# Weight padding split into two ordered steps, a rounding op in four parts, and one more skip on VectorE, in a planned attention + state-space kernel

## The chip, the cores and the metric

The kernel runs on one core of a Trainium2 chip. The metric is device time in microseconds, the median over repeated runs. The engines are TensorE (PE in the profile, with its weight loads as PEld), VectorE (DVE), ScalarE (ACT), GpSimd (POOL) and SyncE (SP); SP issues most of the DMAs. PSUM is where matrix products land; an "evacuation" is the copy of a product from PSUM to SBUF by ACT or DVE.

## The reference, cut to what matters

Two independent layers over 2048 positions of width 448; their outputs stand side by side.

```python
def _A_ref(x, wqkv, wo):                 # attention: each position sees 8 earlier ones, 2 apart
    qkv = (x @ wqkv).reshape(B, S, 3, 16, 28)
    idx = pos[:, None] - (jnp.arange(8) * 2)[None, :]
    logits = einsum("bhsd,bhswd->bhsw", q, k[idx]) * 28 ** -0.5    # masked where idx < 0
    o = einsum("bhsw,bhswd->bhsd", softmax(logits), v[idx])
    return o.reshape(B, S, 448) @ wo

def _B_ref(x, Lambda_re, Lambda_im, B_re, B_im, C_re, C_im, log_dt, Dskip):
    Lam_bar = exp(exp(log_dt) * Lam)                                # complex, 448 states
    for t in range(2048):
        h = Lam_bar * h + Bu[t]                                     # Bu = x @ B_bar
    y = 2.0 * einsum("blp,dp->bld", hseq, Cmat).real + x * Dskip

out = concatenate([A_ref, B_ref], axis=-1)
```

## The kernel before, in words

**Positions go in pairs.** Inputs are viewed as 1024 rows of two positions each (even and odd), 896 numbers wide, and turned so that the width lies on partitions: 7 slabs of 128. With the attention's step of 2, even positions only see even ones and odd only odd. A weight of 448 rows does not divide into slabs of 128, and the two positions of a row start at different partitions, so weights are stored in 7 slabs too, with shifted copies of the same rows in the other 64 partitions (`Wv`, `Wpad`, `wo`); `pair` then runs two matmuls of 64 rows each at once, on upper and lower partitions (lines 546 and 547).

**Steps and their names.** Each step is a node with a name, a cost, its dependencies and a rank. The prediction uses these:

- `vw0..2` build the shifted half of `Wv`; `xt`, `xe` turn the first two blocks of x on PE and copy them out.
- `v0..v7` project V for eight blocks of 128 pairs (`v3_` is the first half of `v3`, four of its seven matmul pairs); `ev0..7` evacuate them.
- `wp{q}{z}` (function `n_wp`, lines 511 to 519) lays the weights of K (q=1) or Q (q=0), half z of the heads, out in 32 columns a head: five copies on one engine, from `Wraw` to `Wpad`. Lines 515 and 516 place the rows, 517 to 519 the copies shifted by 64 partitions.
- `q{q}{s}{c}` projects K or Q for four heads s and chunk c (0: pairs 0 to 255, 1: to 511, 2: to 1023); `eq...` evacuates it.
- `s{par}{b}` scores of block b for even (0) or odd (1) positions, two PSUM units; `x{par}{b}0/1` their exponentials on ACT (line 750); `a{b}` the product with V; `n{b}` the division on DVE.
- `t0`, `tk`, `ts`, `t2`, `t3`, `t4` make the table of sines and cosines: angles on ACT (`t0`), rounding on DVE (`tk`, `ts`), sine on ACT (`t2`), absolute value on DVE (`t3`, line 454), cosine on ACT (`t4`, line 457). The exponentials wait for `t4`.
- `l1`, `l2` scale the B matrices (`wtmp`, `natW`); their transposes by DMA are `WT`.
- `b{hf}{k}` products for one half of the sequence, `be` their evacuation, then on DVE `ma` (line 815), `ri`, `sc` (the scan, line 833), `mb`, `ro` (lines 840, 841): the states h.
- `cg`, `ch` scale C; `g0`, `g1` a Gram-like product `Gm`, evacuated by `ge0`, `ge1`.
- `w0..w7` the attention's output projection. `y{t}` (even) and `z{t}` (odd) the state-space output of block t, `ye` their evacuation, `yo` the store. For t = 4, 5, 6 the odd row's skip term is added on DVE (line 1036) from a product `xd{t}` made beforehand (line 955, from the load `xn` at lines 948 and 949); for the other t it is a matmul with a diagonal. The last odd row is done in two pieces, `z70` (320 columns) and `z71` (128), lines 1014 and 1017.
- `gu1..3` a guard that decides at the end whether a slow exact path runs.

**What sets the order.** `Plan.run` is a list scheduler at build time: it takes the nodes in order of rank, keeps a clock for each engine from the written costs, and gives a free engine the first node that is ready. The result is a fixed order of instructions on each engine, and each engine runs its list in order; real waits are semaphores. So a change of a rank, of a cost or of an earliest time (`at`) moves instructions. PSUM is four units (`mm`), given out in a ring in PE's order: a step needs the unit of the fourth one before it to have been evacuated. A half of `pair` work is followed by a small GpSimd write (`tick`, line 554) that the second half waits for.

Of the kernel before, what the change touches and what calls it, by code (L numbers as in the profile page):

```python
# [23 lines left out]
SCALE = float(DH) ** -0.5  # L24


RANK = {"vi": (-544.75, 131.055), "v": (-110.39, 34.569), "q0": (63.48, 25.419), "q1": (-1326.93, 228.142), "s": (-380.99, 73.488), "a": (-188.15, 159.093),
        "b0": (56.3, -31.172), "b1": (2986.12, -242.123), "d0": (94.79, 241.448), "d1": (1628.45, -108.947), "l": (2486.1, 164.979), "t": (251.37, -53.356),
        "tk": (731.53, 100.376), "xd": (2178.91, -29.053), "cg": (593.37, 8.672), "ch": (1143.63, -50.034), "g": (436.44, 143.698), "y": (468.94, 183.089),
        "w": (1186.02, 1.256), "gu": (1304.36, -293.628), "q2": (430.19, -21.545), "wp": (-27.3, 132.469)}  # L30


class Plan:


    WAKE, TURN = 0.13, 0.1

    def __init__(self, pools):
        self.nodes, self.pools = [], pools
# [177 lines left out]
def kernel(  # L217
# [24 lines left out]
    def t_(shape, dt, name, tag=None):  # L242
        return sb.tile(shape, dt, tag=tag or name, name=name)
# [33 lines left out]
    def xbar_x(dst, src, lo, hi):  # L277
        SP.dma_start_transpose(dst[:, :, lo:hi], src[lo:hi, :])
# [8 lines left out]
    xn_ = [Pb[i][:].rearrange("p a b c -> p (a b c)")[:, 0:2 * D] for i in range(2)]  # L287
    SP.dma_start(xn_[0], xA2[0:128, :])
    ACT.dma_start(Wv[:, 0:3, :], wmain(2))
    ACT.dma_start(Wv[0:64, 3, :], A_wqkv[384:448, 2 * D:3 * D])  # L290
    SP.dma_start(xn_[1], xA2[128:256, :])
    for i, vec in ((2, B_Lambda_im), (3, B_Dskip)):
        G.dma_start(rows[7 * i:7 * i + 7, :], vec.rearrange("(c p) -> c p", p=64))
# [14 lines left out]
    SP.dma_start(Pt[0:64, :], B_B_im[384:448, :])  # L308
    SP.dma_start(Pt[64:128, :], B_B_re[384:448, :])
    xbar_x(xB, xB2, 0, 256)  # L310
    xbar_x(xB, xB2, 256, 512)


    def sel(o, i, pat, op, fill, base, ch):
# [136 lines left out]
        ACT.activation(tab[:, 1], ang, ACTF.Sin, scale=-2 * PI * SHR)  # L451

    def n_t3(e):
        V.tensor_scalar(ang.bitcast(I32), ang.bitcast(I32), 0x7FFFFFFF, None, ALU.bitwise_and)

    def n_t4(e):
        ACT.activation(tab[:, 0], ang, ACTF.Sin, bias=hpi[:], scale=-2 * PI * SHR)
# [33 lines left out]
    def n_vw(e, i):  # L491
        if i == 0:
            V.tensor_copy(Wv[64:128, 4:6, :], Wv[0:64, 1:3, :])
            V.tensor_copy(Wv[64:128, 3, :], Wv[0:64, 0, :])
        elif i == 1:
            V.tensor_copy(Wv[64:128, 6, :], Wv[0:64, 3, :])
        else:
            V.tensor_copy(Wv[0:64, 4:7, :], Wv[64:128, 0:3, :])

    def n_xt(e, i, h):  # L500
        h["ps"] = unit()
        tp = h["tp"] = h["ps"][:].rearrange("p a b -> p (a b)").bitcast(BF16)
        for k in range(7):
            PE.transpose(tp[:, 1024 * (k // 4) + 128 * (k % 4):1024 * (k // 4) + 128 * (k % 4) + 128], xn_[i][:, 128 * k:128 * k + 128], eye[:])
# [6 lines left out]
    def n_wp(e, q, z):  # L511
        o = Wpad[:, :, q, 256 * z:256 * z + 256].rearrange("p k (h c) -> p k h c", c=32)[:, :, :, 0:DH]
        i = Wraw[:, :, D * q + 224 * z:D * q + 224 * z + 224].rearrange("p k (h c) -> p k h c", c=DH)
        f = V.tensor_copy if e == "V" else ACT.copy
        f(o[:, 0:3], i[:, 0:3])
        f(o[0:64, 3], i[0:64, 3])
        f(o[64:128, 3], i[0:64, 0])
        f(o[0:64, 4:7], i[64:128, 0:3])
        f(o[64:128, 4:7], i[0:64, 1:4])

    def evac(e, o, i):
        if e == "A":
            ACT.copy(o, i)  # L523
        else:
            V.tensor_copy(o, i)  # L525
# [58 lines left out]
    late = 18.0  # L584
    gm = []
    for i, f in enumerate(gms):
        gm.append(node(f"gm{i}", {"G": 0.45}, f, gm[-1:], 4))
    g_1 = [node(f"one{a}", {"G": 0.67}, lambda e, a=a: g_one(e, a), [], 10, at=late) for a in range(2)]
    g_z = [node(f"zer{i}", {"G": 0.33 if i < 3 else 0.5}, lambda e, i=i: g_zero(e, i), [], 11, at=late) for i in range(4)]
    g_r = node("rcs", {"G": 0.35}, g_rcs, [], 14, at=late)  # L590
# [21 lines left out]
        tk_ = node(f"tk{k}", {"V": 0.53}, lambda e, k=k: n_tk(e, k), [pB, g_i] + (tss[k - 2:k - 1] if k > 1 else []), ("tk", k))  # L612
        tss.append(node(f"ts{k}", {"V": 0.62}, lambda e, k=k: n_ts(e, k), [t0, tk_], ("t", 0)))
    t2 = node("t2", {"A": 1.9}, n_t2, tss + [e2], ("t", 0))
    t3 = node("t3", {"V": 1.2}, n_t3, [t2], ("t", 0))
    t4 = node("t4", {"A": 2.0}, n_t4, [t3], ("t", 0))
    dg = [node(f"dgO{k}", {"G": 0.5}, lambda e, k=k: g_dgO(e, k), [pD], 15, at=45.0) for k in range(4)]
    for k in range(4):
        dg.append(node(f"dgE{k}", {"G": 0.5}, lambda e, k=k: g_dgE(e, k), [pD] + gm + dg[4:], 15, at=45.0))
    vw = []  # L620
    for i in range(3):
        vw.append(node(f"vw{i}", {"V": (0.48, 0.18, 0.44)[i]}, lambda e, i=i: n_vw(e, i), vw[-1:], (-400, -399, -397)[i], at=(4.5, 5.3, 5.3)[i]))
    xr = []
    for i in range(2):
        h = {}
        x = node(f"xt{i}", {"P": 0.6}, lambda e, i=i, h=h: n_xt(e, i, h), [g_e], -500, alloc="mm", at=(4.3, 5.0)[i])
        xr.append([node(f"xe{i}{z}", {"A": (0.49, 0.37)[z], "V": (0.6, 0.47)[z]}, lambda e, i=i, z=z, h=h: n_xe(e, i, z, h), [x], -398,
                        frees=[(x, 0)]) for z in range(2)])
    wp = {(q, z): node(f"wp{q}{z}", {"V": 1.55, "A": 2.9}, lambda e, q=q, z=z: n_wp(e, q, z), [g_p], ("wp", 2 * z + 1 - q), at=9.7 if q else 11.8)
          for z in range(2) for q in (1, 0)}  # L630


    MS = (0, 4, 1, 5, 2, 6, 3)
# [305 lines left out]


    outv = out[0].rearrange("(t two) n -> t two n", two=2)
    YD = (4, 5, 6)
    sk = {}
    sdone = [n for n in plan.nodes if n["name"][0] == "s" and n["name"][1] in "01"]

    def n_xn(e):
        xo = sk["x"] = t_([128, 4, D], BF16, "xo", "Kt")
        SP.dma_start(xo[:, 0:3, :], B_x[0].rearrange("(b t two) d -> t b two d", two=2, t=128)[:, YD[0]:YD[2] + 1, 1, :])
        SP.dma_start(xo[:, 3, :], B_Dskip.partition_broadcast(128))
    xl = node("xn", {"S": 1.2}, n_xn, sdone, 25, lat=3.0)  # L950
# [34 lines left out]
    for t in range(8):  # L985
# [21 lines left out]
            for k in range(3):  # L1007
                PE.matmul(ps[:, 1, 64 + 128 * k:192 + 128 * k], xB[:, 4 + k, tk], dgO[:, 1 + k, :], start=False, stop=(k == 2), skip_group_check=True)

        def piece(e, lo, n, ds, tk=tk, h=h):  # L1010
            ps, hb = unit(), hbuf(1)
            h["z", lo] = ps
            for m in range(7):
                PE.matmul(ps[:, 1, 0:n], hb[:, m, 385:513], lazy["C1"][:, m, lo:lo + n], start=(m == 0), stop=False, skip_group_check=True)  # L1014
            for k in ds:
                a, b = (0, 64) if k == 0 else (128 * k - 64, 128 * k + 64)
                PE.matmul(ps[:, 1, a - lo:b - lo], xB[:, 3 + k, tk], dgO[:, k, 0:b - a], start=False, stop=(k == ds[-1]), skip_group_check=True)
# [13 lines left out]
        if t < YD[0]:  # L1031
            n2 = node(f"ye{t}", ab(2 * D), lambda e, ev=ev: ev(e, 0, 2), [n1] + qdone, r, frees=[(n0, 0)])
            node(f"yo{t}", {"S": 0.6}, lambda e, st=st: st(e, 0, 2), [n2], 60 + 3 * t, lat=2.2)
        elif t in YD:
            def add(e, t=t, h=h):
                V.tensor_tensor(h["o"][:, 1], h[1][:, 1, 0:D], sk["d"][:, t - YD[0], :], ALU.add)  # L1036
            n2 = node(f"ye{t}0", ab(D), lambda e, ev=ev: ev(e, 0, 1), [n0] + qdone, r, frees=[(n0, 0)])
            n3 = node(f"ye{t}1", {"V": 0.6}, add, [n1, n2, xd[t]], r, frees=[(n0, 0)])
            node(f"yo{t}", {"S": 0.6}, lambda e, st=st: st(e, 0, 2), [n3], 60 + 3 * t, lat=2.2)
        else:  # L1040
            n2 = node(f"ye{t}0", ab(D), lambda e, ev=ev: ev(e, 0, 1), [n0] + qdone, r, frees=[(n0, 0)])
            node(f"yo{t}0", {"S": 0.6}, lambda e, st=st: st(e, 0, 1), [n2], 60 + 3 * t, lat=2.2)
            for i, (lo, n, ds) in enumerate(((0, 320, (0, 1, 2)), (320, 128, (3,)))):
                n0 = n1 = node(f"z{t}{i}", {"P": (1.15, 0.52)[i]}, lambda e, lo=lo, n=n, ds=ds, piece=piece: piece(e, lo, n, ds),
                               [n0] + c1, (r[0], r[1], -0.1), alloc="mm")
                n3 = node(f"ye{t}{1 + i}", {"VA"[i]: (0.42, 0.2)[i]}, lambda e, lo=lo, n=n, h=h: evac(e, h["o"][:, 1, lo:lo + n], h["z", lo][:, 1, 0:n]),
                          [n1, n2], r, frees=[(n1, 0)])
                node(f"yo{t}{1 + i}", {"S": 0.5}, lambda e, lo=lo, n=n, tk=tk, h=h: SP.dma_start(outv[tk, 1, D + lo:D + lo + n], h["o"][:, 1, lo:lo + n]),
                     [n3], 61 + i + 3 * t, lat=2.2)
            g2["deps"].append(n1)  # L1050


    ps = unit()
    for i in range(7):
        PE.matmul(ps[:, 0, :], zz[:, 0:128], zz[:, 128:640], start=True, stop=True)
    plan.run({"P": 4.3, "A": 4.5, "V": 1.0, "S": 23.2, "G": 2.7})
    bad = nc.values_load(flag[0:1, 0:1])
    main.close()
    with tc.If(bad > 0, label="exact"):
# [31 lines left out]
```

## Time and profile before

| what | value |
|---|---|
| median of 13 runs | 134.47 us (134.07 to 136.32) |
| the profiled execution's own time | 134.16 us |
| its span | 132.4 us, so 1.76 us lie around it |
| PE busy | 126.1 us, 95% |
| DVE busy | 107.6 us, 81% |
| ACT busy | 90.2 us, 68% |
| POOL busy | 27.7 us, 21% |
| granted TensorE clock | 0.997 |

The profiled execution is 0.31 us below the median. A sum made from the profile is a difference against 134.16, and is carried over to the median unchanged. Busy shares are averages: what bounds a stage is read from the waits and the timeline of that stage. Matmuls are pipelined, so a stretch in which PE is shown busy can still hold small gaps between the starts of its rows.

### The profile page before, as it was taken

To read this page: it belongs to the slowest core of one execution; us is meant where nothing else is said; L and a number is where in the kernel's file an instruction comes from. 1 tells how busy PE (TensorE), PEld (TensorE's weight loads), DVE (VectorE), ACT (ScalarE), POOL (GpSimd) and SP (SyncE) were. 2 spreads that over 40 slices of the span, in tenths; PEclk is the share of its full clock that TensorE was granted. 3 is DMA by queue.
4 is the path that set the end of the run, shared out by engine and by line. 5 is a ranking of instruction groups with operands and counts; after the bars stand their busy time and mean duration, and the time that the engine had idled before them with its cause. 6 is when DMAs were issued, how large, how long until landed. Compare 5 with 4: busy or idle time off the path is not lost.

```text
span 132.4 us, 3803 instructions
## 1 busy us (share of the span) xinstructions
PE 126.1 (95%) x1533; PEld 70.9 (54%) x1533; DVE 107.6 (81%) x193; ACT 90.2 (68%) x121; POOL 27.7 (21%) x108
## 2 busy tenths in 40 slices
PE   5899999999999999999999999999999999999980
PEld 2455766786445454545454554655675655455550
DVE  0439999899879999999999999999999899921130
ACT  0539899989998956999999899834775266211120
POOL 6975146210899600000000000000000000000000
PEclk9999999999999999999999999999999999999998
DMA  4999989609848999442505123379346669442231
GB/s 78 310 261 224 214 185 231 121 7 114 168 81 150 186 182 127 100 115 42 130 5 111 21 63 75 107 225 119 107 99 175 146 66 296 139 139 74 69 104 45
DMA packets 42432, 17.26 MB, mean 130 GB/s; under 512 B 33452, under 2 KB 42412, under 8 KB 42412
## 3 DMA queue, kind: packets, MB, share of 16 engines
q1 hardware_dynamic: 41840, 16.58, 60.1%
q10 hardware_dynamic: 508, 0.40, 1.0%
q8 instruction: 13, 0.21, 0.6%
q14 instruction: 7, 0.06, 0.1%
q0 software_dynamic: 64, 0.00, 0.0%
HBM read 4.08 MB, written 3.67 MB: 58 GB/s over the span
## 4 chain that ended last, share of the span: by engine, by line
PE 86%; DMA 3%; ACT 3%; DVE 2%; issue 1%; POOL 0%; SPq 0%; POOLq 0%; ACTq 0%
PE mm L546 28%; PE mm L804 17%; PE mm L996 8%; PE mm L1003 7%; PE mm L763 5%; PE mm L998 5%; PE mm L895 4%; PE mm L740 4%; PE mm L547 3%; DMA P<-in_A_x_dram 3%; PE mm L744 3%; PE mm L1014 1%; ACT wtmp L529 1%; DVE Va L525 1%; ACT P L750 1%
## 5 line engine op out<-in xcount | busy, mean ns | idle before, releaser
L750 ACT ACTIVATE P<-mm 128x896 bf16<-128x896 f32 (+1 forms) x36 | 31.5, 929 | 2.1 <-PE mm L744 1.9
L546 PE MATMUL mm<-xA,Wpad 64*128 64x256 bf16 (+1 forms) x168 | 27.2, 305 | 0.4 <-POOL tick L554 0.4
L547 PE MATMUL mm<-xA,Wpad 64*128 64x256 bf16 (+1 forms) x168 | 27.2, 306 | 0.1
L523 ACT CAST ys<-mm 128x896 bf16<-128x896 f32 (+2 forms) x15 | 11.3, 765 | 23.1 <-PE mm L1003 8.9
L804 PE MATMUL mm<-xB,WT 128*128 128x512 bf16 x98 | 22.5, 379 | 0.2 <-PE mm L744 0.2
L554 POOL MEMSET tick<- 1x1 f32 x40 | 4.8, 120 | 83.6 <-PE mm L547 83.4
L546 PEld LDWEIGHTS <-Wpad 64*128 64x128 bf16 x168 | 14.9, 94 | 8.9 <-POOL tick L554 1.4
L547 PEld LDWEIGHTS <-Wpad 64*128 64x128 bf16 x168 | 14.7, 94 | 1.2 <-issue 0.5
L804 PEld LDWEIGHTS <-WT 128*128 128x128 bf16 x98 | 9.1, 97 | 10.8 <-issue 0.7
L546 PE MATMUL mm<-Wv,xA 64*128 64x448 bf16 x56 | 12.5, 350 | 0.0
L547 PE MATMUL mm<-Wv,xA 64*128 64x448 bf16 x56 | 12.4, 350 | 0.0
L996 PE MATMUL mm<-C,h 128*128 128x448 bf16 x56 | 11.9, 353 | 0.0
L546 PE MATMUL mm<-wo,OT 64*128 64x448 bf16 x56 | 10.8, 349 | 0.0
L547 PE MATMUL mm<-wo,OT 64*128 64x448 bf16 x56 | 10.8, 349 | 0.0
L1003 PE MATMUL mm<-C,h 128*128 128x448 bf16 x49 | 10.4, 353 | 0.0
L770 DVE TENSOR_TENSOR O<-mm,rcs 112x896 bf16<-112x896 f32 (+1 forms) x9 | 9.8, 1091 | 0.3
L523 ACT CAST u<-mm 128x1024 bf16<-128x1024 f32 (+1 forms) x8 | 7.2, 903 | 3.2 <-PE mm L804 3.2
L833 DVE TENSOR_TENSOR_SCAN rs<-p_r,ini,rv 128x512 bf16<-128x512 f32 x7 | 8.7, 1270 | 0.0
L833 DVE TENSOR_TENSOR_SCAN rs<-p_r,rv 128x512 bf16<-128x512 f32 x7 | 8.5, 1230 | 0.0
L763 PEld LDWEIGHTS <-P 128*128 128x128 bf16 x288 | 7.9, 96 | 1.0 <-issue 0.4
L1036 DVE TENSOR_TENSOR ys<-mm,xd 128x448 bf16<-128x448 f32 x3 | 1.9, 625 | 8.1 <-ACT ys L523 8.1
L815 DVE TENSOR_TENSOR ra<-u,tab 128x2048 bf16<-128x2048 bf16 x6 | 7.3, 1221 | 0.7 <-DVE h L841 0.5
(178 smaller groups left out, 242.5 us busy)
## 6 DMA issues: line engine op xcount, KB each, us to landing
out_dram<-ys SPq DMA_DIRECT2D x15, 224.0 KB, 2.4
Wraw<-in_A_wqkv_dram SPq DMA_DIRECT2D x2, 336.0 KB, 4.0
wo<-in_A_wo_dram SPq DMA_DIRECT2D x2, 336.0 KB, 3.1
P<-in_A_x_dram SPq DMA_DIRECT2D x2, 224.0 KB, 3.7
vw<-Va SPq DMA_DIRECT2D x2, 203.0 KB, 3.7
vw<-Va SPq DMA_DIRECT2D x2, 174.0 KB, 3.2
Wv<-in_A_wqkv_dram ACTq DMA_DIRECT2D x1, 336.0 KB, 4.0
natW<-in_B_B_re_dram SPq DMA_DIRECT2D x1, 336.0 KB, 4.8
```

Source lines behind the costliest of these rows:

```text
L523: ACT.copy(o, i)
L546: x = PE.matmul(ps[:, a, 0:n], lhs(0, lo[i]), rhs(0, lo[i]), start=(i == 0), stop=(i == 6), skip_group_check=True)
L547: y = PE.matmul(ps[:, b, 0:n], lhs(64, hi[i]), rhs(64, hi[i]), start=(i == 0), stop=(i == 6), skip_group_check=True)
L750: ACT.activation(P[:].rearrange("p s g q -> p g s q")[:, 2 * z:2 * z + 2, :, 0:n], h["s"][z][:, :, 0:4 * n].rearrange("p g (s q) -> p g s ...
L763: PE.matmul(av[:, par, 29 * hd:29 * hd + 29], hb_[par]["P"][:, hd // 4, hd % 4, :], v[:, par, hd, :], start=True, stop=True)
L770: V.tensor_tensor(O[0:n, :].rearrange("p (a h d) -> p a h d", a=2, h=H), avv[0:n, :, :, 0:DH], rc.unsqueeze(3).to_broadcast((n, 2, H, DH)) ...
L804: PE.matmul(ps[:, i, :], WT[:, j, 128 * m:128 * m + 128], xB[:, j, HALF * hf:HALF * hf + HALF], start=(j == 0), stop=(j == 6))
L815: V.tensor_tensor(a[:], x[:].unsqueeze(1).to_broadcast((128, 2, 2, HALF)), tab[:, :, k, :].unsqueeze(2).to_broadcast((128, 2, 2, HALF)), A ...
L833: V.tensor_tensor_scan(h["s"][:, i], p["r2"][:, k:k + 1].to_broadcast((128, HALF)), h["v"][:, i], 0.0 if hf == 0 else ini[:, m:m + 1], ALU ...
L996: PE.matmul(ps[:, 0, 0:D], hb[:, m, lo:lo + 128], lazy["C2"][:, m, :], start=(m == 0), stop=False, skip_group_check=True)
L998: PE.matmul(ps[:, 0, 0:D], xB[:, k, tk], Gm[:, k, :], start=False, stop=(k == 3), skip_group_check=True)
L1003: PE.matmul(ps[:, 1, 0:D], hb[:, m, lo + 1:lo + 129], lazy["C1"][:, m, :], start=(m == 0), stop=(t in YD and m == 6), skip_group_check=True)
```

## The change

1. `n_wp` keeps the two copies that place the rows; a new function `n_ws` makes the three shifted copies from `Wpad` itself, in runs of 256 columns, padding included, as a node of its own that follows its padding and may run on the other engine.
2. `n_t3` becomes four instructions, one for each 512 columns.
3. The odd skip of block 7 goes to DVE: a fourth row in the load `xn`, a product `xd7`, two additions with `xd7` in place of two copies, and no diagonal matmuls in `piece`. The last store is issued by ACT, not by SP.
4. The last 64 rows of `Wv` are loaded through POOL's queue, ahead of its other loads, not through ACT's; one transposing load of 256 rows becomes two of 128.
5. All ranks, some costs and earliest times and the planner's wake-up cost differ, and a table `FINE` adds an offset to the rank of about 240 single nodes. Through these the order of nearly every engine's list moves.

```diff
-RANK = {"vi": (-544.75, 131.055), "v": (-110.39, 34.569), ...
+RANK = {"vi": (-6211.57, 311.074), "v": (-394.68, 85.971), ...
+FINE = {"t0": -138.5, "tk0": -130.6, "ts0": 246.9, ...
-    WAKE, TURN = 0.13, 0.1
+    WAKE, TURN = 0.18, 0.1
...
-    ACT.dma_start(Wv[0:64, 3, :], A_wqkv[384:448, 2 * D:3 * D])
+    G.dma_start(Wv[0:64, 3, :], A_wqkv[384:448, 2 * D:3 * D])
...
-    xbar_x(xB, xB2, 256, 512)
+    xbar_x(xB, xB2, 256, 384)
+    xbar_x(xB, xB2, 384, 512)
...
     def n_t3(e):
-        V.tensor_scalar(ang.bitcast(I32), ang.bitcast(I32), 0x7FFFFFFF, None, ALU.bitwise_and)
+        for k in range(4):
+            V.tensor_scalar(ang[:, k].bitcast(I32), ang[:, k].bitcast(I32), 0x7FFFFFFF, None, ALU.bitwise_and)
...
         f(o[:, 0:3], i[:, 0:3])
         f(o[0:64, 3], i[0:64, 3])
-        f(o[64:128, 3], i[0:64, 0])
-        f(o[0:64, 4:7], i[64:128, 0:3])
-        f(o[64:128, 4:7], i[0:64, 1:4])
+
+    def n_ws(e, q, z):
+        w = Wpad[:, :, q, 256 * z:256 * z + 256]
+        f = V.tensor_copy if e == "V" else ACT.copy
+        f(w[64:128, 3], w[0:64, 0])
+        f(w[0:64, 4:7], w[64:128, 0:3])
+        f(w[64:128, 4:7], w[0:64, 1:4])
...
+            if name in FINE:
+                rank = rank[:2] + ((rank[2] if len(rank) == 3 else 0) + FINE[name],)
...
-    t3 = node("t3", {"V": 1.2}, n_t3, [t2], ("t", 0))
+    t3 = node("t3", {"V": 1.4}, n_t3, [t2], ("t", 0))
...
-YD = (4, 5, 6)
+YD = (4, 5, 6, 7)
...
-        def piece(e, lo, n, ds, tk=tk, h=h):
+        def piece(e, lo, n, h=h):
...
-                PE.matmul(ps[:, 1, 0:n], hb[:, m, 385:513], lazy["C1"][:, m, lo:lo + n], start=(m == 0), stop=False, skip_group_check=True)
-            for k in ds:
-                a, b = (0, 64) if k == 0 else (128 * k - 64, 128 * k + 64)
-                PE.matmul(ps[:, 1, a - lo:b - lo], xB[:, 3 + k, tk], dgO[:, k, 0:b - a], start=False, stop=(k == ds[-1]), skip_group_check=True)
+                PE.matmul(ps[:, 1, 0:n], hb[:, m, 385:513], lazy["C1"][:, m, lo:lo + n], start=(m == 0), stop=(m == 6), skip_group_check=True)
...
+                def add(e, lo=lo, n=n, h=h):
+                    V.tensor_tensor(h["o"][:, 1, lo:lo + n], h["z", lo][:, 1, 0:n], sk["d"][:, 3, lo:lo + n], ALU.add)
+                def put(e, lo=lo, n=n, tk=tk, h=h):
+                    (ACT if e == "A" else SP).dma_start(outv[tk, 1, D + lo:D + lo + n], h["o"][:, 1, lo:lo + n])
...
-    plan.run({"P": 4.3, "A": 4.5, "V": 1.0, "S": 23.2, "G": 2.7})
+    plan.run({"P": 4.3, "A": 4.5, "V": 1.0, "S": 23.2, "G": 3.15})
```

The order that the planner makes of the changed kernel, where it matters most (underscore: first half):

```
PE before:   v0 v1 v2 v3_ tr v3 q121_ q121 q101_ q111_ q101 v4_ q111 q131_ ...
PE after:    v0 v1 v2 v4_ q101_ q111_ v4 q101 q111 tr v5_ q121_ q131_ v5 ...
DVE before:  ... xe11 ev1 wp11 ev2 pA pD pB eq101 ...    ts0 ts1 tk2 ts2 tk3 ts3 l20 eq120 l24 eq020 t3 ...
DVE after:   ... xe11 wp10 ws10 ev2 wp00 ev4 eq101 ...   ts1 tk3 ts3 ts0 eq110 tk2 ts2 l24 ev7 l21 l15 l12 t3 ...
ACT before:  xe00 xe10 ev0 wp10 ev3 e1 eq121 wp00 ...    t4 x000 x001 l16 be00 x100 x101 ...
ACT after:   xe00 xe01 xe10 ev0 ev1 wp11 ws11 eq111 ws00 ...   t4 x000 x001 be00 x010 x011 eq112 ...
```

## The prediction

> **What bounds the kernel now.** I read the page's busy table and slices first, then the waits, then DVE's busy time by stretches, and last the timeline at four places.
>
> ```profile
> PE 126.1 (95%) x1533; PEld 70.9 (54%) x1533; DVE 107.6 (81%) x193; ACT 90.2 (68%) x121; POOL 27.7 (21%) x108
> PE   5899999999999999999999999999999999999980
> DVE  0439999899879999999999999999999899921130
> ACT  0539899989998956999999899834775266211120
> ```
>
> PE is full from slice 2 to 38, but so is DVE from slice 3 to 34, and ACT to slice 26. PE's row gives it hardly a wait; its slack is in starts that lie apart.
>
> ```profile
> 12.03 0.35 PE L546 MATMUL mm<-Wv,xA 64*128 64x448 bf16 x1
> 12.04 0.35 PE L547 MATMUL mm<-Wv,xA 64*128 64x448 bf16 x1
> 12.22 0.27 PE L546 MATMUL mm<-xA,Wpad 64*128 64x256 bf16 x1
> 12.59 0.28 PE L547 MATMUL mm<-xA,Wpad 64*128 64x256 bf16 x1
> ...
> 12.93 0.27 PE L547 MATMUL mm<-xA,Wpad 64*128 64x256 bf16 x1
> 13.47 0.28 PE L546 MATMUL mm<-xA,Wpad 64*128 64x256 bf16 x1 [0.27 <-POOL tick L554]
> ```
>
> A pair of 256 columns takes 0.11 us (12.71 to 12.82), one of 448 takes 0.19 (12.03 to 12.22). So 12.22 to 12.59 holds a gap of 0.26 (the first pair waits for line 519 on DVE, ending 12.54), and 12.93 to 13.47 one of 0.43 (a second half waits for its tick). With 0.40 at 23.2 and small ones PE loses some 1.2 us before 36 us. Between 57.4 and 62.3 the same reading gives another 1.2 (0.13, 0.19, 0.11, 0.52, 0.24).
>
> ```profile
> 9.54:36.17 26.63, 26.10 (x364) 17.48 (x360) 24.96 (x63) 25.37 (x41) 9.72 (x49) 1.00 0.83 159
> 36.17:57.00 20.83, 20.68 (x269) 10.13 (x271) 19.70 (x31) 17.02 (x20) 9.45 (x26) 1.00 0.90 136
> 57.00:84.00 27.00, 26.93 (x374) 14.09 (x366) 26.30 (x44) 24.77 (x34) 0.18 (x2) 1.00 0.30 67
> 84.00:112.75 28.75, 28.75 (x388) 16.74 (x386) 27.79 (x42) 16.72 (x20) 0.61 (x6) 1.00 0.65 154
> ```
>
> Columns: stretch, length, then busy time of PE, PEld, DVE, ACT, POOL. DVE is busy 98.75 of 103.21 us, from its first evacuation to its last state. Of the 4.46 idle, its waits name 2.0; the rest are seams between instructions.
>
> ```profile
> 112.33 0.42 DVE L841 TENSOR_TENSOR h<-ra 128x512 bf16<-128x512 bf16 x1
> 114.63 1.50 PE L996 MATMUL mm<-C,h 128*128 128x448 bf16 x7
> ```
>
> Line 996 at 114.63 is y4, the first product that needs all states; the last is written at 112.75. DVE is thus only 1.9 us ahead of PE at the gate to the last 14 us. **PE bounds, with DVE close behind.**
>
> **What the skill says.** The Trainium skill, SBUF — State Buffer, "SBUF: two separate sides", says that a two-port DVE instruction and a GpSimd instruction lock each other out. The trace fits: line 515 took 0.93 us at 19.12 beside a POOL memset, against 0.39 at 10.66. The same box says a DMA issued from POOL can be held up by such DVE work; POOL's two loads landed 4.7 and 4.8 us after issue, the ACT load that moves there 4.8, so no penalty shows. The skill, ScalarE: Activation LUTs, "What ACT_TABLE_LOAD costs", gives 186 + 0.833·N ns for an instruction without pointer operands: 746 for 672 columns, where the trace has 750. I use it for the shifted copies on ACT.
>
> **The change, part by part.**
>
> *Padding and shift.* Before, DVE does two whole copies (10.66 to 12.54, and 19.12 to 21.20): 3.96 us. The planner's order gives DVE three paddings and two shifts. A padding is lines 515 and 516: 0.39+0.35 early, 0.93+0.19 late, 0.74 to 1.12. A shift is one copy of 256 columns and two of 768, bracketed by line 496 (448 columns, 0.27), line 518 (672, 0.39 to 0.53) and line 498 (1344, 0.54): about 0.2+0.42+0.42, 1.05. Sum 3×0.93+2×1.05 = 4.9: **DVE +0.95**. ACT goes from two whole copies of 2.95 (9.77 to 12.71) to one padding (1.04 by start) and two shifts of 0.40+0.83+0.83 by the skill's formula (estimate): 5.2 against 5.9, −0.7. What it buys: DVE no longer takes ev1 first, so wp10 can start at about 9.5 (ACT already read Wraw at 9.77), and is whole at 9.5+0.74+1.05 = 11.3. PE, after v0 to v2 and half of v4 (3×1.31+0.75 from 6.28), gets there at 11.0. The gap of 0.26 mostly goes, and pairs of first halves put work over the ticks (0.43 and 0.40). Late next: v5_ takes the PSUM unit of v4, whose evacuation stands on DVE behind ws10, ev2 and wp00: 11.3+1.1+0.74+1.1 = 14.2 against PE at 13.4, so 0.8 comes back there.
>
> *Rounding in four parts.* Line 454 takes 1.21 for 2048; tiny fp32 steps take 0.165, so by that line a quarter is 0.165+0.51 per thousand × 512 = 0.43, or 0.35 by start. Four: 1.4 to 1.7, **DVE +0.3**. t4 still waits for all four.
>
> *Moved DVE work.* In the new order DVE makes five of the l1 products, not three (2×0.53 = **+1.06**), none of the Gm evacuation (0.62+0.61, 1.14 with overlap: **−1.2**), and xd4 before the last state (**+0.61**). Evacuations of V, K and Q stay 3, 7 and 3.
>
> DVE before the gate: 0.95+0.3+1.06−1.2+0.61 = +1.7. Against it stand the named 2.0 us of waits, which a better order can use: last state between 112.75+1.7−2.0 = 112.4 and 114.4, middle 113.4. So **y4 at about 113.5, −1.1 us**. PE gets there if it keeps 1.1 net: 1.2 early, less 0.8, plus some of the 1.2 at 57 to 62, where the new order spreads the Q and K chunks between scores. That is the cap I take.
>
> *Tail.* The diagonal matmuls of block 7 go: 0.14+0.07 (chain, line 1017) = 0.2 on PE.
>
> ```profile
> 128.23 0.49 DVE L525 CAST ys<-mm 128x320 bf16<-128x320 f32 x1 [1.94 <-PE mm L1017]
> ...
> 128.68 0.27 ACT L523 CAST ys<-mm 128x128 bf16<-128x128 f32 x1 [0.96 <-PE mm L1017]
> 128.75 0.82 SPq L1048 DMA_DIRECT2D out_dram<-ys  x2
> ```
>
> The addition of 320 takes about the copy's 0.49 (line 1036: 0.625 for 448), from 128.09 to 128.58; that of 128 about 0.3, to 128.88 (ACT: 128.95). Both now queue on DVE, and the flag behind them: 0.1 later. SP's second issue, at 129.2 behind the first, goes to ACT at about 128.95; SP reads the flag at 129.05, not 129.6. Landing is 1.5 after issue: 130.45 for 130.7. **Tail −0.25 to −0.55, take −0.4.**
>
> *Loads and the rest, taken at 0, ±0.3.* Wv's last rows leave ACT's queue (0.53 of issue; the table load behind it waits on nothing PE needs before 5.28) for the head of POOL's. There two row loads (needed by tr at 11.5), the eye (done 3.2, needed 4.29), the padding memset (done 4.0, needed 9.5), the masks (needed at 33.8) slip by one issue, 0.53 to 0.79. vw1 stood at 6.28 before; it now stands ahead of xe11 in DVE's list, so a late load holds vw2 and v0's second half. One more transpose issue costs SP about 0.45 (1.24 each for 128 rows, 4.03 for two of 256) ahead of the V windows and C loads; SP idles from 25.4 to 29.07. The load for xd grows by a row and has 8 us of cover. The last store's issue on ACT has only the flag behind it.
>
> **Sum:** −1.1−0.4 = −1.5. On the profiled 134.16 that is 132.66; on the median of 134.47, **133.0**.
>
> **The rivals.** *A, as above:* 133.0, own range 132.0 to 134.1, chance 0.52. *B, the order also packs DVE fully:* the last state at 112.4, y4 −2.1, tail −0.55: 131.8. For it: PE has 2.4 us of gaps. Against: seams and waits never all go. 0.20. *C, slower: the exponentials start late.*
>
> ```profile
> 30.76 1.21 DVE L454 TENSOR_SCALAR tmpB<-tmpB 128x2048 int32<-128x2048 int32 x1
> 32.84 2.02 ACT L457 ACTIVATE tab<-tmpB,p_hpi 128x2048 bf16<-128x2048 f32 x1
> 34.88 1.28 ACT L750 ACT_TABLE_LOAD   x1
> 36.17 1.94 ACT L750 ACTIVATE P<-mm 128x1024 bf16<-128x1024 f32 x2
> ```
>
> x000, at 36.17, frees its unit at about 37.1; PE needs it for its next scores at 38.2. So 1.1 us of delay are free, and each one beyond is PE's. In the new list l24, ev7, l21, l15 and l12 stand between the last ts and t3 (0.6+1.0+0.6+0.5+0.45 = 3.2; before, 28.45 to 30.76, 2.3), t3 is 0.3 longer, and the ts come three evacuations and an l2 later, against an earlier start: t3 may end at 34.0, not 31.97, and t4 start 1.2 late, at that very point. If it is 2 us late, PE loses 1 and DVE's states as much: 134.47+1.0−0.4 = 135.1. 0.20. *D, nothing changes:* the early gains are given back at v5_ and at the gate, only the tail shows, against a small loss: 134.4. 0.08.
>
> **How the numbers follow.** About 0.2% (0.27 us) is what a measurement of this kernel can tell from no change. Faster: A and B, 0.72. Same: 0.08. Slower: C, 0.20. The range leaves out the outer part of B and of C: 131.4 to 135.1.
>
> **What would show it.** In the profile after: no gap before the first K pair, one of up to 0.8 near 13.4 at a V block; x000 between 36 and 37.4; the last line for h near 113.4 and y4 right behind it; the time from PE's last row to the end of the span (128.73 to 132.4 now, 3.7) shorter by 0.2 to 0.4. I am wrong if y4 follows PE's own w7 with DVE long done (then PE, not DVE, set the gain), or if x000 comes after 37.4 and PE waits for line 750's units.

## The result, and the profile after

The changed kernel takes **135.29 us** (median of 11 runs, 134.74 to 135.91). The kernel before, timed beside it, takes 134.34 us (48 runs). The ratio is 1.007, 95% interval 1.0055 to 1.0085: slower by 0.95 us. The forecast was 133.0, faster. The profiled execution of the changed kernel took 135.62 us, with a span of 133.8. That is 1.46 us above the profiled execution before (134.16), where the medians are 0.95 apart: some 0.5 us of what the two traces differ by is scatter of single executions, and a difference read between them is a place, not an exact price.

The busy line and the slices of the page after:

```profile
PE 125.9 (94%) x1529; PEld 72.7 (54%) x1529; DVE 107.6 (80%) x198; ACT 90.1 (67%) x120; POOL 30.8 (23%) x109
...
PE   6899897999989999999998999999999999999990
...
DVE  0547979999977999999999899999999999811130
ACT  3419999949999585978999799788357256601120
```

DVE's total is 107.6 us, as before, and the totals of PE and ACT are lower by 0.2 and 0.1. What has changed is in the slices: PE has a 7 in its seventh (20.1 to 23.4 us) where it had a 9, and ACT has a 4 in its ninth (26.8 to 30.1) where it had an 8. The totals say nothing of that.

The timeline at the places that the prediction named, with what ended a wait in brackets:

```profile
14.34 0.35 PE L582 MATMUL mm<-Wv,xA 64*128 64x448 bf16 x1 [0.40 <-DVE Va L561]
...
17.48 0.89 ACT L559 CAST Va<-mm 128x896 bf16<-128x896 f32 x1
18.43 0.27 PE L582 MATMUL mm<-xA,Wpad 64*128 64x256 bf16 x1 [0.29 <-ACT Va L559]
...
20.81 1.17 DVE L476 TENSOR_SCALAR tmpB<-tmpB,p_f 128x512 f32<-128x512 f32 x2
21.90 1.27 DVE L561 CAST Qt<-mm 128x512 bf16<-128x512 f32 x2
22.63 0.27 PE L582 MATMUL mm<-xA,Wpad 64*128 64x256 bf16 x1 [0.87 <-DVE Qt L561]
...
30.09 0.91 ACT L559 CAST Va<-mm 128x896 bf16<-128x896 f32 x1 [1.50 <-PE mm L583]
30.89 1.91 ACT L482 ACTIVATE tab<-tmpB 128x2048 bf16<-128x2048 f32 x1
33.00 1.43 DVE L486 TENSOR_SCALAR tmpB<-tmpB 128x512 int32<-128x512 int32 x4
34.45 0.40 PE L781 MATMUL mm<-msk 32*128 32x512 bf16 x4
34.60 2.00 ACT L489 ACTIVATE tab<-tmpB,p_hpi 128x2048 bf16<-128x2048 f32 x1
37.92 1.94 ACT L791 ACTIVATE P<-mm 128x1024 bf16<-128x1024 f32 x2
39.91 0.37 PE L582 MATMUL mm<-xA,Wpad 64*128 64x512 bf16 x1 [0.35 <-ACT P L791]
40.80 1.23 DVE L856 TENSOR_TENSOR ra<-u,tab 128x2048 bf16<-128x2048 bf16 x1 [1.54 <-ACT u L559]
...
114.25 0.42 DVE L882 TENSOR_TENSOR h<-ra 128x512 bf16<-128x512 bf16 x1
...
116.44 1.50 PE L1037 MATMUL mm<-C,h 128*128 128x448 bf16 x7
```

and the first scores of the kernel before:

```profile
33.71 0.40 PE L740 MATMUL mm<-msk 32*128 32x512 bf16 x4
```

Read it from top to bottom. At 18.43 PE waits for the evacuation of a V block on ACT, which stands behind the two shifts that ACT now makes (12.52 to 14.62 and 15.25 to 17.35); by the starts of its rows PE loses 0.46 us there. At 22.63 `q021_` waits for the evacuation `eq001`, which stands on DVE behind the shift `ws01` (19.50 to 20.80) and the rounding steps `tk0`, `tk1`; by the starts of its rows PE loses 1.05 us there. First scores come at 34.45, 0.74 us later than before (33.71). The last rounding step on DVE ends at 30.17, where it ended at 28.45 before; `t2` starts at 30.89, behind `ev3` on ACT, and x000 at 37.92, which is 1.75 later than the 36.17 of before. At 40.80 DVE waits 1.54 us for the first evacuation of the state-space part, which stands behind the exponentials. y4 at 116.44 is 1.81 later than before. The last state is written at 114.67, 1.77 ahead of it: DVE is as far ahead of this gate as it was (1.88). PE followed its own attention output projection.

The tail after:

```profile
129.90 0.69 DVE L1083 TENSOR_TENSOR ys<-mm,xd 128x320 bf16<-128x320 f32 x2 [1.80 <-PE mm L1055]
130.41 0.34 SPq L1086 DMA_DIRECT2D out_dram<-ys  x1
...
130.62 0.38 ACTq L1086 DMA_DIRECT2D out_dram<-ys  x1
```

Both additions take 0.69 us on DVE, and the two stores leave from two queues 0.21 us apart. From y4 to the end of the span it is 17.36 us (133.8 − 116.44), against 17.77 (132.4 − 114.63): −0.41.

### The profile page after: what moved, and what is told of

Read it like the earlier page. It is cut to its first block, busy times and chain, and to the rows that moved or that the text cites. A ratio compares the mean times of both kernels' runs of the same rounds, so it can differ in the third digit from the quotient of the medians.

```text
span 133.8 us, 3796 instructions
## 1 busy us (share of the span) xinstructions
PE 125.9 (94%) x1529; PEld 72.7 (54%) x1529; DVE 107.6 (80%) x198; ACT 90.1 (67%) x120; POOL 30.8 (23%) x109
## 4 chain that ended last, share of the span: by engine, by line
PE 63%; DVE 22%; DMA 5%; ACT 4%; issue 2%; SPq 0%; DVEq 0%
PE mm L582 19%; PE mm L1037 8%; PE mm L1044 7%; PE mm L583 5%; PE mm L845 5%; PE mm L1039 5%; PE mm L936 4%; PE mm L804 4%; DVE O L811 3%; DMA P<-in_A_x_dram 3%; DVE C L916 3%; DVE ra L856 3%; DVE rs L874 3%; PE mm L781 3%; DMA OT<-O 2%
## 5 line engine op out<-in xcount | busy, mean ns | idle before, releaser
L582 PE MATMUL mm<-xA,Wpad 64*128 64x256 bf16 (+1 forms) x168 | 26.8, 304 | 1.5 <-DVE Qt L561 0.9
L583 PE MATMUL mm<-xA,Wpad 64*128 64x256 bf16 (+1 forms) x168 | 26.8, 305 | 0.0
L559 ACT CAST ys<-mm 128x896 bf16<-128x896 f32 (+1 forms) x15 | 11.8, 807 | 20.9 <-PE mm L1044 8.9
L590 POOL MEMSET tick<- 1x1 f32 x40 | 4.1, 102 | 82.4 <-PE mm L583 82.3
L582 PEld LDWEIGHTS <-Wpad 64*128 64x128 bf16 x168 | 15.4, 94 | 5.9
L583 PEld LDWEIGHTS <-Wpad 64*128 64x128 bf16 x168 | 14.9, 94 | 2.6 <-issue 2.2
L582 PE MATMUL mm<-Wv,xA 64*128 64x448 bf16 x56 | 11.9, 349 | 0.4 <-DVE Va L561 0.4
L583 PE MATMUL mm<-Wv,xA 64*128 64x448 bf16 x56 | 11.9, 350 | 0.0
```

The source lines that it names most:

```text
L582: x = PE.matmul(ps[:, a, 0:n], lhs(0, lo[i]), rhs(0, lo[i]), start=(i == 0), stop=(i == 6), skip_group_check=True)
L583: y = PE.matmul(ps[:, b, 0:n], lhs(64, hi[i]), rhs(64, hi[i]), start=(i == 0), stop=(i == 6), skip_group_check=True)
```

## The experiments

Three theories were stated at first. **T1:** the order of the lists costs the time, in single waits of PE. **T2:** the new forms of the instructions cost it. **T3:** the late exponentials alone, the prediction's rival C. Two more came later. **T4:** DVE's whole load from 19 to 33 us bounds PE there. **T5:** against it, that ACT is as full there. Medians stand beside the kernel before on the same chip, which took 134.27 to 134.41. Most runs have 4 to 7 executions, and an interval reaches some 0.2 us to either side, so the gains below are known to a few tenths. Single traces also start apart: in the new order the first V product comes anywhere between 6.03 and 6.51 us. Where two traces are compared, that offset is to be taken off.

### Parts of the change in the old order

*forms_in_old_order:* before, with the last three lines of `n_wp` reading from `Wpad`, and line 454 in four parts.

```diff
-        f(o[64:128, 3], i[0:64, 0])
-        f(o[0:64, 4:7], i[64:128, 0:3])
-        f(o[64:128, 4:7], i[0:64, 1:4])
+        w = Wpad[:, :, q, 256 * z:256 * z + 256]
+        f(w[64:128, 3], w[0:64, 0])
+        f(w[0:64, 4:7], w[64:128, 0:3])
+        f(w[64:128, 4:7], w[0:64, 1:4])
...
-        V.tensor_scalar(ang.bitcast(I32), ang.bitcast(I32), 0x7FFFFFFF, None, ALU.bitwise_and)
+        for k in range(4):
+            V.tensor_scalar(ang[:, k].bitcast(I32), ang[:, k].bitcast(I32), 0x7FFFFFFF, None, ALU.bitwise_and)
```

> Order of before, with two forms of the change alone: the shifted copies taken from Wpad in runs of 256 columns (inside the old node), and the rounding in four parts. T1 (the new order costs the time, the forms next to nothing): 134.2 to 134.7, within 0.3 us of before; the four parts take 1.43 us for 1.21 on DVE, x000 moves by 0.2 to 0.3 and its unit has slack. T2 (the forms themselves cost the 0.95 us): 135.0 to 135.4.

Measured: 134.65, ratio 1.0029 (1.0016 to 1.0042). A loss of 0.3 us, at the upper edge of what T1 allowed and a third of what T2 needs. Its timeline shows one place where PE pays, first as it was before and then in this run:

```profile
45.53 0.81 PE L804 MATMUL mm<-xB,WT 128*128 128x512 bf16 x3 [0.15 <-PE mm L744]
```

```profile
45.84 0.38 PE L806 MATMUL mm<-xB,WT 128*128 128x512 bf16 x1 [0.35 <-DVE O L772]
```

PE waits for the division `n0` on DVE, which came 0.31 us later than before (44.60 for 44.29), and the product starts 0.31 later too; before, its only named wait was 0.15 us for PE's own work. Of the 0.31, 0.11 was there already at first scores (33.82 for 33.71) and stayed 0.11 up to the fourth scores (44.92 for 44.81), so PE loses 0.20 at this place. A delay of DVE thus counts at 45.8, long before the gate at 112.

*tail_in_old_order:* before, with the third edit alone (`YD = (4, 5, 6, 7)`, `xd7`, two additions on DVE, no diagonal in `piece`, the last store from ACT).

> Before with the whole tail part alone (fourth row in the skip's load, xd7, two additions on DVE, no diagonal matmuls in the last pieces, last store issued by ACT). The prediction's step: -0.4 us, 134.0 for 134.34, the time from y4 to the span's end 17.36 for 17.77. A rival: xd7 and the two additions delay DVE's states or the final copies, 134.3 or more.

Measured: 133.95, ratio 0.9972 (0.9958 to 0.9986): −0.40 us. The prediction's step said −0.4: it holds, and this part of the change is a gain.

*new_order_old_forms:* the changed kernel, with the first diff of this section taken the other way round (inside `n_ws` and `n_t3`), the order of every list kept.

> The changed kernel with its order of instructions kept, but the rounding again one instruction and the shifted copies again taken from Wraw in runs of 224 (tail as changed). T1: 135.1 to 135.3, as slow as the changed kernel. T2: back to about 134.3.

Measured: 134.85, ratio 1.0040 (1.0022 to 1.0057). Between the two: 0.44 us under the changed kernel. Neither T1 nor T2 alone. This kernel differs from tail_in_old_order by its order, with the split nodes and the moved loads: 134.85 − 133.95 = +0.90. So the loss divides into −0.40 for the tail, +0.90 for order and loads together, and +0.44 for the forms in the new order. These are steps from one kernel to the next, so that they sum to the whole is no test of them. The loads were not run apart from the order.

*one_rounding:* the changed kernel, with only the rounding again as one instruction.

> The changed kernel with the rounding t3 as one instruction for its four parts, all else kept. If t3's 0.22 us is what the two forms together cost in the changed kernel (0.44 us), 134.9 to 135.05; if the shifted copies from Wpad carry it, 135.2 to 135.35.

Measured: 135.47, ratio 1.0079 (1.0065 to 1.0094). No gain, so the four parts are not what the 0.44 is. That leaves the shifted copies, by elimination: they were not run alone. In the changed kernel `ws01` takes 0.43, 0.42 and 0.42 us on DVE; with the old form it took 0.21, 0.39 and 0.39, was done 0.28 earlier, and `q021_` started at 22.36 for 22.63. On ACT the old form takes 0.38, 0.75 and 0.75 for each of two shifts, against 0.40, 0.83 and 0.83, and the wait at 18.43 is not there. At first scores 0.19 of all this is left (34.26 for 34.45). In these two traces 0.28 more comes at a4, near 73 us, whose wait for a load is shorter there (0.24 for 0.53); that wait also differs among runs that keep the new forms (see a4_later), so this part need not belong to the forms.

### The late exponentials

*cosine_twice:* before, `t4` issued twice, which delays ACT alone.

```diff
-        ACT.activation(tab[:, 0], ang, ACTF.Sin, bias=hpi[:], scale=-2 * PI * SHR)
+        for k in range(2):
+            ACT.activation(tab[:, 0], ang, ACTF.Sin, bias=hpi[:], scale=-2 * PI * SHR)
```

> Before with the cosine step t4 issued twice on ACT (2.0 us more on ACT alone, the same result written again): x000 goes from 36.17 to about 38.2, later than in the changed kernel (37.92). T3 (late exponentials alone carry the loss, with 1.1 us of slack as the prediction's rival C has it): +0.9 us or more, 135.2 up. T1 (the loss lies earlier, and late exponentials cost only the 0.35 us seen at 39.91): +0.2 to +0.5, about 134.7.

Measured: 136.67, ratio 1.0175 (1.0161 to 1.0188), +2.3 us: in T3's range, which had no upper end, and far above T1's. The timeline:

```profile
38.31 1.94 ACT L751 ACTIVATE P<-mm 128x1024 bf16<-128x1024 f32 x2
...
39.38 0.40 PE L741 MATMUL mm<-msk 32*128 32x512 bf16 x4 [1.01 <-ACT P L751]
40.30 1.89 PE L805 MATMUL mm<-xB,WT 128*128 128x512 bf16 x8 [0.29 <-ACT P L751]
40.84 1.43 DVE L648 SCALAR_TENSOR_TENSOR natW<-natW,p_a,wtmp 128x448 bf16<-128x448 bf16 x1 [2.59 <-ACT wtmp L530]
...
47.96 0.38 PE L805 MATMUL mm<-xB,WT 128*128 128x512 bf16 x1 [1.06 <-DVE O L771]
```

x000 is 2.14 us late, second scores 1.18 (39.38 for 38.20). So 0.96 us was free, close to the 1.1 that rival C read off. But the bill goes on: 0.35 more by the third scores, and 0.9 more by the fifth, because DVE stood still for 2.59 us behind an `l1` product on ACT, and then came late with `n0`. A late ACT is paid twice, once in PSUM units and once through DVE.

*half_cosine:* the changed kernel with half of `t4`. It leaves out half of the cosines, so its states are other numbers than the reference's, and ACT has about 1 us less to do.

```diff
-        ACT.activation(tab[:, 0], ang, ACTF.Sin, bias=hpi[:], scale=-2 * PI * SHR)
+        G.memset(tab[:, 0, 2:4], 0.0)
+        ACT.activation(tab[:, 0, 0:2], ang[:, 0:2], ACTF.Sin, bias=hpi[:], scale=-2 * PI * SHR)
```

> The changed kernel with t4 computing the cosines of half the columns alone (the other half set to zero on GpSimd, so the states are not the reference's): t4 takes about 1.05 us for 2.00 and x000 comes at 36.9 to 37.0 for 37.92. T1 (the exponentials' delay costs only what is seen at 39.91): the gap of 0.35 goes, 134.9 to 135.1. T3: all of 0.95 us comes back, 134.3.

Measured: 134.71, ratio 1.0034 (1.0021 to 1.0047): 0.58 us of the 0.95 come back. T1 had said 0.2 to 0.4, T3 all.

```profile
37.14 1.94 ACT L792 ACTIVATE P<-mm 128x1024 bf16<-128x1024 f32 x2
...
39.46 0.39 PE L583 MATMUL mm<-xA,Wpad 64*128 64x512 bf16 x1
...
40.11 1.23 DVE L857 TENSOR_TENSOR ra<-u,tab 128x2048 bf16<-128x2048 bf16 x1 [0.78 <-ACT u L560]
```

The wait of `q112_` at 39.91 is gone (39.46, no bracket), and DVE waits 0.78 for 1.54. From second to third scores PE needs 2.98 us, not 3.44, and from fifth to sixth 2.24, not 2.43. Together that is 0.65. The late exponentials are a real part of the loss, and rival C's mechanism with it. They are not all of it: in this kernel first scores still came at 34.53.

### Single waits of PE

*qk_evac_first:* the changed kernel with three nodes moved in the finished order: `ws01` behind `eq011`, then `tk0`, then `tk1`.

> The changed kernel with one place of VectorE's list altered: the evacuations eq001 and eq011 stand ahead of the shift ws01 and the rounding steps tk0, tk1 (in the changed kernel behind them), so that q021_ at 22.63 need not wait. T1 (PE starves where evacuations stand behind other VectorE work): the gap of 1.05 us goes, first scores at 33.4 to 33.7 for 34.45; the exponentials, bound by the ts steps and ev3, come forward by less, so some 0.3 is given back at the units of line 791; 134.4 to 134.8 for 135.29. T3 (the late x000 alone sets the loss): no better than 135.0, since x000 hardly moves.

Measured: 136.64, ratio 1.0169 (1.0149 to 1.0189). The move made it worse, for `q021_` needs not only the unit of `eq001`, but the shifted half that `ws01` writes. The run says nothing of T1 or T3.

```profile
23.48 0.28 PE L590 MATMUL mm<-xA,Wpad 64*128 64x256 bf16 x1 [1.80 <-DVE Wpad L562]
```

In the changed kernel the bracket named `eq001` alone. A wait names only what came last; here another stood right behind it.

*tk_behind_evac:* the same with `ws01` left in place; only `tk0` and `tk1` go behind `eq011`.

> The changed kernel with only the rounding steps tk0 and tk1 moved behind the evacuations eq001 and eq011 on VectorE (the shift ws01, which q021_ needs, stays where it is). T1: q021_ starts about 1.0 us earlier (21.6 for 22.63), first scores at about 33.5; t2 is then bound by the ts steps at 30.2 and x000 comes at about 37.2, so of 1.0 us some 0.3 is lost again at line 791's units: 134.4 to 134.8. Below nothing: the ts chain on VectorE slips by its new place and x000 does not move, 135.0 to 135.3.

Measured: 135.63, ratio 1.0098 (1.0083 to 1.0113): no gain at all, and above both ranges expected.

```profile
25.53 0.35 PE L589 MATMUL mm<-Wv,xA 64*128 64x448 bf16 x1 [0.99 <-DVE Qt L568]
...
34.61 0.40 PE L788 MATMUL mm<-msk 32*128 32x512 bf16 x4
```

The gap of 1.05 at 22.63 is gone, and one of 1.17 stands at 25.53, where `v6_` waits for the next Q evacuation, `eq020`. First scores come at 34.61, no sooner. T1 in its simple form falls here: what is taken from one place of DVE's list is owed at the next.

*v4_evac_first:* the changed kernel with `wp00` moved behind `ev4`, for the gap at 14.34.

> The changed kernel with the padding wp00 moved behind the evacuation ev4 on VectorE, so that v5_ at 14.34 has its unit in time. T1: the gap of 0.58 us goes and first scores come 0.3 to 0.6 earlier unless ws00 or the Q pairs become late; 134.7 to 135.1. T3: 135.3, no change. Below nothing: wp00 is late for ws00 and the first Q pair waits, 135.3 to 135.6.

Measured: 135.48, ratio 1.0082 (1.0061 to 1.0102), no change, against T1. The timeline tells why:

```profile
13.12 1.09 DVE L568 CAST Va<-mm 128x896 bf16<-128x896 f32 x1 [1.10 <-PE mm L590]
...
14.27 0.35 PE L589 MATMUL mm<-Wv,xA 64*128 64x448 bf16 x1 [0.40 <-DVE Va L568]
```

DVE was idle for 1.10 us before `ev4`: it waited for v4 to end. The wait of `v5_` comes from PE's own order: v4, whose second half comes behind the first halves of two K chunks, ends only at 13.1, and its unit is wanted one evacuation and a few short products later.

*a4_later:* the changed kernel with `a4` moved behind `s05` on PE. In the changed kernel:

```profile
69.53 0.51 SPq L736 DMA_DIRECT2D vw<-Va  x1
...
70.10 1.55 SPq L737 DMA_DIRECT2D vw<-Va  x1
...
73.66 0.50 PE L804 MATMUL mm<-vw,P 128*128 128x29 bf16 x14 [0.53 <-DVE ra L856]
```

The window `vw` has one buffer, and its load can be issued only when a3 has read it. Before, a4 stood 7.80 us behind a3; in the new order it stands 5.12 behind. The bracket names DVE's line 856, of which a4 uses nothing; in new_order_old_forms the same wait is put down to the load:

```profile
73.18 0.96 PE L805 MATMUL mm<-vw,P 128*128 128x29 bf16 x32 [0.24 <-DMA vw<-Va]
```

> The changed kernel with the product a4 moved behind the scores s05 on PE, so that its window of V, loaded only after a3 has read the one buffer, has 1.1 us more to land. T1: the gap ahead of a4 at 73.66 goes, 0.4 to 0.6 us, if the exponentials of s05 do not wait; 134.7 to 134.9. Rival: PE is gated later by the chain of VectorE's states, so the gain is given back by the last projection, 135.2 to 135.3.

Measured: 134.78, ratio 1.0040 (1.0024 to 1.0055): −0.51 us, as T1 said, and no wait is left ahead of a4. This one was a single wait. Its length is not fixed. In the other traces of the new order in which a4 keeps its place it runs from none (tk_behind_evac) to 0.64 us (one_rounding), and it is longest where SP's second issue for the window takes longest (1.29 us with a wait of 0.24, 1.55 with 0.53, 1.67 with 0.64).

*three_mended:* the changed kernel with the old forms, `tk0`, `tk1` and `a4` moved.

> The changed kernel with old forms (one rounding instruction, shifts taken from Wraw), tk0 and tk1 behind eq001 and eq011, and a4 behind s05. T1, by adding what each did or is to do (-0.44, -0.5 to -0.9, -0.5): 133.5 to 133.9, at or under the kernel with the tail alone (133.95). If the places share one bound, less: 134.2 to 134.5.

Measured: 134.62, ratio 1.0018 (1.0008 to 1.0027). That is above both ranges expected, since the move of `tk0` and `tk1` was taken for a gain. With what each part had measured alone, −0.44, −0.51 and +0.34, the sum is 134.68: within the noise the parts add.

### DVE's load from 19 to 33 us

Busy time in the two stretches (length, then PE, PEld, DVE, ACT, POOL with their instructions, clock, DMA share, GB/s), of the kernel before:

```profile
19.50:26.00 6.50, 6.35 (x98) 4.63 (x96) 6.29 (x17) 6.26 (x11) 3.09 (x13) 1.00 0.91 186
26.00:33.00 7.00, 7.00 (x112) 5.25 (x108) 6.37 (x11) 6.53 (x11) 0.69 (x8) 1.00 0.54 64
```

and of the changed kernel:

```profile
19.50:26.00 6.50, 5.63 (x100) 5.16 (x97) 6.39 (x16) 6.32 (x13) 3.18 (x13) 1.00 0.99 163
26.00:33.00 7.00, 7.00 (x96) 5.07 (x94) 6.82 (x12) 4.92 (x6) 0.81 (x7) 1.00 0.44 80
```

DVE is busy 13.21 of 13.50 us in the changed kernel (12.66 before), while ACT has dropped from 6.53 to 4.92 in the second stretch. Between 20 and 26 us the new order has four Q evacuations on DVE (21.90 to 25.92), where the old one had two, and ACT then waits 1.9 us for PE. PE falls short in the first stretch alone (5.63 of 6.50 us); in the second it is busy for all 7.00 in both kernels. ACT, too, is busy for 6.32 of 6.50 in the first stretch; its room lies in the second.

*q_evac_on_scalar:* the changed kernel with one of the four on ACT.

```diff
+        for n in order:
+            if n["name"] in ('eq001',):
+                n["by"] = "A"
         for n in order:
             n["fn"](n["by"])
```

> The changed kernel with one evacuation, eq001 (0.65 us on VectorE), done by ScalarE at the same place of the order. T4 (VectorE's load from 19 to 33 us bounds the new order there, whatever stands first in its list): q021_ starts at about 21.8 for 22.63 and no gap takes its place, first scores 0.5 to 0.7 us earlier (33.8), x000 likewise; 134.6 to 134.8. T5 (ScalarE is as full as VectorE there, so that eq120, eq010 and t0 are late in turn): 135.2 or more.

Measured: 134.88, ratio 1.0039 (1.0025 to 1.0052): −0.41 us.

```profile
33.52 0.39 PE L784 MATMUL mm<-msk 32*128 32x512 bf16 x4
```

```profile
19.50:26.00 6.50, 6.48 (x109) 5.64 (x106) 6.33 (x16) 6.49 (x13) 2.71 (x13) 1.00 1.23 143
26.00:33.00 7.00, 7.00 (x90) 4.24 (x86) 6.44 (x13) 5.53 (x8) 0.72 (x6) 1.00 0.67 102
```

PE is busy 6.48 in the stretch, not 5.63, and no gap takes the place of the old one. First scores come at 33.52, 0.93 earlier, but 0.40 of that is the start of this execution: its first V product stands at 6.04 for 6.44, and DVE is 0.40 early at `ws01` (19.10 for 19.50), before the edit can act. The edit is thus worth 0.53 at first scores, near the 0.5 to 0.7 that T4 expected, and 0.33 at x000 (37.19 for 37.92, less the 0.40). The median lies just above T4's range and well under T5's 135.2. So T4 holds for the stretch from 19.5 to 26 us and T5 falls, although ACT was as full by its busy share. The wait at 39.91 (now at 39.18) and a4's are still there.

*shift_twice:* before, with the three shifted copies of `wp01` issued twice on DVE.

```diff
         f(o[64:128, 4:7], i[0:64, 1:4])
+        if (q, z) == (0, 1):
+            f(o[64:128, 3], i[0:64, 0])
+            f(o[0:64, 4:7], i[64:128, 0:3])
+            f(o[64:128, 4:7], i[0:64, 1:4])
```

> Before with the three shifted copies of wp01 (Q, second half of the heads; on VectorE at 20.18 to 21.20) issued twice, 1.0 us more on VectorE at that place, the same values written again. If VectorE has room there in the old order: 134.3 to 134.6, the wait of 0.53 at 26.57 shrinks. If VectorE's time at that place is PE's time in the old order too: 135.0 to 135.4.

Measured: 136.00, ratio 1.0129 (1.0114 to 1.0144), +1.7 us. The extra copies took longer than I had reckoned:

```profile
20.41 0.39 DVE L518 COPY Wpad<-Wraw 64x672 bf16<-64x672 bf16 x1
20.84 0.60 DVE L519 COPY Wpad<-Wraw 64x672 bf16<-64x672 bf16 x1
21.36 0.28 DVE L521 COPY Wpad<-Wraw 64x224 bf16<-64x224 bf16 x1
21.68 0.67 DVE L522 COPY Wpad<-Wraw 64x672 bf16<-64x672 bf16 x1
22.38 0.39 DVE L523 COPY Wpad<-Wraw 64x672 bf16<-64x672 bf16 x1
...
22.82 0.28 PE L551 MATMUL mm<-xA,Wpad 64*128 64x256 bf16 x1 [1.39 <-DVE Wpad L523]
```

The shifts end at 22.77, not 21.20, and first scores come 1.62 later (35.33): one for one. PE waits here for the shift itself, so what the run shows is that in the old order this shift has no room: delayed by DVE's time, it delays PE by as much. The views of before did not call it a bound, because the shift just kept pace: it ended at 21.20, PE used it at 21.25, and no wait had a length.

*two_on_scalar:* the changed kernel with the old forms, `a4` moved, and `eq001` and `eq110` on ACT.

> The changed kernel with old forms and a4 behind s05, and two evacuations, eq001 and eq110, done by ScalarE. T4, by adding: 134.85 for the old forms, -0.5 for a4, -0.5 to -0.8 for VectorE's 1.3 us less: 133.5 to 133.9, first scores near 33.5. T5: 134.3 or more, no better than the two mended places alone.

Measured: **133.65**, ratio 0.9948 (0.9935 to 0.9961). First scores at 33.45, x000 at 36.92. That is 0.6 us faster than before and 1.6 faster than the changed kernel, inside T4's range, and the lowest median of all that ran. The tail's 0.40 is in it, so the kernel to set beside it is tail_in_old_order (0.9972, 0.9958 to 0.9986): the two intervals just touch. The new order with its three faults mended is no worse than the old one; that it is better is not shown.

## Why the prediction was wrong

**The bound.** I read "PE bounds, with DVE close behind" off the gate at y4, where DVE is 1.9 us ahead, and booked all of DVE's extra work (+1.7) against that gate and against the 2.0 us of its named waits. This is the step that failed. DVE's work is not due at 112 us as one sum. Its evacuations, shifts and divisions are due one by one: at 21 us (shift_twice, one for one), at 22.6 or 25.5 (tk_behind_evac, 1.05 us of PE at the one or 1.17 at the other), at 45.8 (forms_in_old_order, 0.20). At the gate itself the margin is still 1.8 us in the changed kernel. Both signs of being wrong that the prediction named are there: y4 follows PE's own w7, with DVE done before it, and x000 comes at 37.92 with PE waiting for its unit at 39.91. The sum was off as well: up to its last state DVE is busy 102.28 us, against 101.44 before, so +0.84 and not +1.7.

**PE's early gain**, the cap that I took ("1.2 early, less 0.8"): the two gaps that I named behaved as forecast. No gap stands before the first K pair (it starts at 11.56, where I had reckoned 11.0), and one of 0.58 stands at 14.34 (up to 0.8 forecast), though for another reason than I gave: not `wp00`, but the late end of v4. What I did not look for was a new gap at 22.63. I wrote "Evacuations of V, K and Q stay 3, 7 and 3": true as a count (three of V, seven of K or Q at 512 columns, three at 1024), and the wrong question. Four of the seven stand between 20 and 26 us, beside the new shift. The gap at 18.43, behind the shifts on ACT, was not looked for either: the prediction booked those shifts as ACT's own −0.7. First scores came 0.74 later instead of about 0.4 earlier.

**y4 at −1.1** was measured at +1.81 in the traces; by the medians, with the tail's 0.40 taken out, it is about +1.35. The 1.81 is made of 0.74 by first scores, 0.41 more by the scores of 62.77 (61.62 before), and 0.66 from there to the output projection, in which the late V window of a4 has a part.

**Rival C** was the right kind of case with too small a chance. Its reading of the slack held: 0.96 us free for 1.1 (cosine_twice). `t4` started 1.76 late (34.60 for 32.84), between the 1.2 that it read off and the 2 that its sum was made with, and x000 came 1.75 late. What it lacked: PE was late by 0.74 itself, so that x000 stood at the edge of the slack for second scores, and the cost appeared one unit later, at x001, and on DVE at 40.80. Its sum of 135.1 is near the 135.29 measured. It comes out so partly by chance, since the shifts and a4, which it does not hold, carry part of the loss.

**Sizes.** t3 in four parts: 1.43 us, 1.4 to 1.7 forecast, and no cost in time that one_rounding can tell. Padding on DVE: 0.85, 0.69 and 0.56 us by busy time, 0.93 taken for each. Shift on DVE: 1.18 and 1.27 us, 1.05 taken, and it stands straight ahead of PE; with the paddings the sum is 4.55, under the 4.9 taken. Shift on ACT: 0.40, 0.83 and 0.83, as the estimate by the Trainium skill's page ScalarE: Activation LUTs, "What ACT_TABLE_LOAD costs", had them: 186 + 0.833·N ns gives 0.40 for 256 columns and 0.83 for 768. Moved loads at nothing: not shown. In the trace after, DVE waits 0.18 us at 5.76 for the last rows of `Wv`, which come through POOL's queue now (0.36 and 0.37 in two other runs of the new order), and the first V product starts at 6.44 for 6.28. Tail: −0.41 in the trace and −0.40 alone, −0.4 forecast.

**Still open:** how the forms' 0.44 divides between the shifts on ACT, that on DVE and the changing wait at a4; what the moved loads cost (two_on_scalar keeps them and does not stand above tail_in_old_order, so they can hardly be most of the loss); and how much each of the evacuation `eq001`, a4 and the exponentials would bring beside the others. Alone they brought 0.41, 0.51 and 0.58. These are not shares of the order's 0.90: half_cosine leaves out work that the kernel needs, and two_on_scalar won back more than was lost.

## What to carry to other kernels

Where each engine works through a fixed list, an item that PE needs has a due time of its own, and not one at the end. Before work is added to such a list, look at what PE uses next in that stretch and how far ahead of its use each item ends: here a shift ended 0.05 us before its use, no wait had a length, and 1.57 us more of it cost 1.62 at first scores.

When a reordered list is to be priced, count the items of each engine by stretch and not over the whole run. A wait that is mended alone and comes back at the next item (1.05 us, then 1.17) means that the list is owed more than one item; moving an item to another engine was then the edit that helped, and swapping it within the list was not. A busy share alone does not say which engine has room: from 19.5 to 26 us DVE was busy for 6.39 and ACT for 6.32 of 6.50 us, and ACT could still take an evacuation, since it waited for PE right after.

## What was not expected of the hardware

DVE copies of one shape took 0.39 or 0.60 to 0.67 us in the same kernel (64x672, shift_twice). The long ones ran while POOL was filling memory: its memsets of `P` stood at 20.54 to 21.58 and that of `Gm` at 21.64 to 22.11, and the copies at 20.84 and 21.68 start under them, while that at 20.41 began before them and that at 22.38 after them. `tk0` and `tk1` fit as well: 1.17 us for two at 20.81 under such memsets in the changed kernel, 0.87 at 22.46 in tk_behind_evac. But in the kernel before the copy at 20.81, of the same line and under the same memsets of `P`, took 0.39. So to start under a memset goes with a longer copy in most places and not in all, and what decides it is not shown; no run moved the memsets. The prediction had quoted the lock between the two engines for one row and taken a mean of a slow and a fast padding, but priced the shift and the rounding without it.
